# Query and value loads behind the block writes, a substitution begun in parts, and z in two pieces: a delta-rule layer with a maxout network on one core

## The chip, the core and the metric

The kernel runs on one core of a Trainium2 chip. Its time is the device time of one execution in microseconds (us); the number given for a kernel is the median of its runs. Profiles are taken by the hardware profiler on one execution. The engines are PE (TensorE; PEld is its weight load), DVE (VectorE), ACT (ScalarE), POOL (GpSimd) and SP (SyncE, which only issues DMAs). "L443" is line 443 of the kernel before. A change of 1% of the time (5 us) is about what a measurement of this kernel can tell from none.

## What is computed

Two layers one after the other. The first is a recurrence over 768 tokens for 4 batches x 8 heads, with a 48 x 48 state for each head (a delta rule); the second is a feed-forward network on its 3072 output rows of 384 numbers. In float32:

```python
k_n = k / (np.linalg.norm(k, axis=-1, keepdims=True) + 1e-06)
state = np.zeros((B, H, D, D), dtype=np.float32)
for t in range(S):
    kt, vt, bt = (k_n[:, :, t], v[:, :, t], beta[:, :, t, None])
    y[:, :, t] = np.einsum('bhd,bhde->bhe', q[:, :, t], state)
    v_old = np.einsum('bhde,bhd->bhe', state, kt)
    state = state + bt[:, :, :, None] * np.einsum('bhd,bhe->bhde', kt, vt - v_old)
...
x = y.transpose(0, 2, 1, 3).reshape(B * S, H * D)
h = np.maximum(np.maximum(x @ w1, x @ w2), x @ w3)     # 384 -> 768
return (h @ w_out).astype(np.float32)                  # 768 -> 384
```

## The kernel before, in words

**Chunks, units, groups.** The tokens are cut into 12 chunks of 64. A chunk has two units (one for each parity of the batch index; a unit holds 2 batches x 8 heads), so there are 24 units n = 0 to 23, and 6 groups m of two chunks each (512 tokens, four units). Inside a chunk the recurrence is solved in closed form: with the products of keys A = k k^T of a unit, a lower triangular system in blocks has to be inverted. Its 32 x 32 diagonal blocks are inverted by forward substitution on VectorE, for all blocks of a group at once, one block per partition; the rest is joined by small matmuls.

**Names of the steps.** For a unit n: `turn` (t, or T for queries alone) transposes keys and queries on TensorE (L366) and copies them out (L372); `gram` (g, or P for the products with queries alone) forms the products of keys and queries (L443); `to_dram` writes the key products to a scratch tensor at_d as eight block writes for two units (L473); `masked` (M) masks the query products (L427). For a group m: `blocks` gathers at_d with one block per partition (L544); `solve` runs the substitution; a run of it is advanced by hand, with one `yield` between its parts, as `some(solving, n)`, or S in the lists below. For a chunk c: `halves_z` and `halves_u` (e, f; only for the first two chunks, in 16 x 16 pieces), `turn_t1` (d, transposes on VectorE, L685 and L687), `join_z` (z, L768) and `join_u` (j, L781) complete the inverse `ut`; `old_k` (k, L798 and L810) and `old_q` (q, L798 and L818) apply the state; `new` (u, L826) forms the new values; `step` (s, L849 and L856) updates the state; `to_y` (y, L868 and L870) and `to_x` (x, L887) give the rows for the network. `scale` multiplies a chunk's values by the key norms (L324).

**The substitution** (L559 to 661). After the diagonal's inverse square root (L278 to L283) and the scaling by beta (L582), L599 scales the whole block matrix; the `yield` behind it ends the first part. Then come 31 steps j with two VectorE instructions each (L617 and L621), and one `yield` after each. For group 1 the result goes to the scratch tensor y_d (L641, two writes, one for each chunk) and is read back into `ut` in eight reads (L653, four for each chunk).

**Weights.** Each of 24 pieces is fetched as raw 64-bit words (`fetch`, L224, into five buffers), changed to float32 by three ScalarE instructions (L255 to L257, two sets of buffers), one on VectorE (L266) and one on POOL (L270, called by `join_last` or by the next piece).

**What sets the order.** Nothing is scheduled automatically: `tc.manual_schedule()` holds for the whole program, so each engine runs its instructions in the order in which the Python code makes them, and waits come from data and from buffers. The start-up (L1390 to L1472) handles group 0's keys and first chunk by hand. Then the network of group 0 is a generator, `ffn(0)`: each of its first 30 steps is one p_h, three accumulating products on 256 tokens (L1311, two passes each), followed by ScalarE (L1319, L1321) or VectorE (L1325); it has two buffers in PSUM. The body of the loop from L1558 runs after step i and hangs the other work there: the lists `FIRST` (chunk 1 and the solving of group 1), `EARLY_LINKS` (group 1), `SOLVED`, `FETCHED`, `CONVERTED` and `LESS`, in that order of calls. PSUM has three more buffers, `ps_two`, for all small products.

**The lines that the change touches.** `load_v(1)` stands at L1462 and is issued by POOL behind the weight fetch of L1461; `scale(1)` at L1562, in the body after step 0, with POOL; `load_q` for units 4 to 6 at L1564 to L1567, after steps 1 and 2, with SP. A q load writes one of three slots (`qpad[n % 3]`), so units 4, 5 and 6 go where units 1, 2 and 3 (the last in slot 0) were; their last readers are the transposes `turn(1..3, (1,))` of L1430 to L1435. `v_t` has three buffers.

Of the kernel before, what the change touches and what calls it, by code (L numbers as in the profile page):

```python
# [23 lines left out]
def kernel(  # L24
# [31 lines left out]
    nc = tc.nc  # L56
# [69 lines left out]
    def load(src, dst, n, queues):  # L126
        c, g = divmod(n, 2)
        for bb in range(2):
            queues[bb].dma_start(
                out=dst[rows(bb ^ g), :, 0:D],  # L130
                in_=src[2 * bb + g, :, c * C : (c + 1) * C, :].rearrange(
                    "h p d -> p h d"
                ),
            )
# [7 lines left out]
    def load_q(n, queues=one_queue):  # L142
        load(q, qpad[n % NQ], n, queues)

    def load_v(c, queue=nc.sync):
        vts[c] = work.tile([128, 2, H, D], FP32, name="v_t", bufs=3)
        for bb in range(2):
            queue.dma_start(  # L148
                out=vts[c][rows(bb)].rearrange("p g h d -> p (g h) d"),
                in_=v[2 * bb : 2 * bb + 2, :, c * C : (c + 1) * C, :].rearrange(  # L150
                    "b h p d -> p (b h) d"
                ),
            )
# [78 lines left out]
    def join_last():  # L232
        if waiting:
            joined(*waiting.pop())
# [88 lines left out]
    def scale(c, nrm):  # L323
        (nc.vector if c > 9 else nc.gpsimd).tensor_tensor(  # L324
            out=vts[c], in0=vts[c],
            in1=nrm[:, :, :, None].to_broadcast([128, 2, H, D]), op=ALU.mult,
        )
# [7 lines left out]
    nrm_0 = const.tile([128, 2, 2, H], FP32, name="nrm_0")  # L335
# [96 lines left out]
    def gram(n, parts=(0, 1), queues=one_queue, copy=nc.scalar.copy, later=False):  # L432
        kqt, g = kqts[n], n % 2
        p_g = ps_two("p_g")

        whole = len(parts) == 2 and not g
        for j in range(NP):
            for par in range(2):
                for bb in range(2):
                    kq = kqt[dims(par), j, bb ^ g]  # L440
                    for i in (0,) if whole else parts:
                        c0 = j * 128 + i * C
                        nc.tensor.matmul(  # L443
                            p_g[
                                rows(bb ^ (g * i)), par, c0 : c0 + C * (1 + whole)
                            ],
                            kq[:, 0],
                            kq if whole else kq[:, i],
                        )
        p_v = p_g.rearrange("p two (j i t) -> p two j i t", j=NP, i=2)  # L450
        if 1 in parts:
            pt = pts[n] = square("pt")
            if later:
                return lambda: copy(by_par(pt), p_v[:, :, :, 1])
            else:
                masked(pt, p_v[:, :, :, 1])
        if 0 not in parts:
            return
        at = ats[n] = square("at")
        copy(by_par(at), p_v[:, :, :, 0])  # L460
        if queues:
            to_dram(n, queues)
# [96 lines left out]
    def solve(m):  # L559
# [34 lines left out]
        else:  # L594
            size, xv, yv = BL, x[:, None], y[:, None]
            xb, by = x, bl[:, None, :].to_broadcast([128, BL, BL])
        if m == 2:
            yield
        nc.vector.tensor_tensor(out=xb, in0=xb, in1=by, op=ALU.mult)  # L599
        yield  # L600
        for j in range(size - 1):
# [5 lines left out]
            n = BL // size  # L607
# [86 lines left out]
    def halves_t(c, parts=(0, 1)):  # L694
        if c not in fine:
            fine[c] = [square("t") for g in range(2)]
        src = [ut[c % NU][:, g].rearrange("p h x -> p (h x)") for g in range(2)]
        dst = [t.rearrange("p h x -> p (h x)") for t in fine[c]]
        if 0 in parts:
            nc.vector.transpose(out=dst[0], in_=src[0])  # L700
        for bb in range(2) if 1 in parts else ():
            nc.vector.transpose(out=dst[1][rows(1 - bb)], in_=src[1][rows(bb)])
# [665 lines left out]
    def some(gen, n):  # L1368
        for _ in range(n):
            if next(gen, gen) is gen:  # L1370
                break
# [62 lines left out]
    some(conv, 1)  # L1434
    turn(3, (1,))  # L1435
    scores = [gram(n, (1,), None, later=True) for n in (2, 3)]
    some(solving, HB + 1)
    for copied in scores:
        copied()
# [15 lines left out]
    for n in range(2):  # L1455
# [3 lines left out]
    new(0)  # L1459
    some(conv, 1)  # L1460
    fetch(nc.gpsimd)  # L1461
    load_v(1, nc.gpsimd)  # L1462
    placed(1, 3)
    to_y(0)
    busy(2, ident)
    join_last()
    halves_t(1)
    solving = solve(1)
    some(solving, 1)
    to_x(0)  # L1470
# [27 lines left out]
    }  # L1498
    EARLY_LINKS = {
        9: "k0 q0", 10: "t0", 11: "t1", 12: "g0", 13: "t2", 14: "g1", 15: "t3",  # L1500
        16: "g2", 17: "g3", 20: "d0 d1 z0 z1", 22: "j0", 24: "j1 u0", 26: "s0",
        27: "y0", 28: "k1 q1", 29: "u1", 30: "s1 x0", 31: "y1",
    }


    FIRST = {
        0: "S1 S1", 1: "e1 s0 S1 S1 S1", 2: "f1 k1 M2 S1 S1",
        3: "z1 d1 S1 M3 S1 S1", 4: "j1 q1", 5: "u1 T4", 6: "y1 s1 T5", 7: "x1 T6",
        8: "T7", 14: "P4", 15: "P5", 23: "P6", 25: "P7", 30: "P9 P11",
    }  # L1510


# [26 lines left out]
    def queries(names):  # L1539
# [12 lines left out]
    FETCHED = {8: 1, 12: 1, 13: 1, 14: 1, 21: 2, 22: 1, 23: 1, 24: 1, 25: 1}  # L1552
    LESS = {3: 0, 6: 1, 9: 2, 18: 3, 21: 4, 25: 5}
    SOLVED = {
        **{i + 4: n for i, n in enumerate((3, 2, 2, 2, 3, 3, 3, 3, 2, 2))},
        27: 1, 28: 1, 29: 1, 30: 6, 31: 17, 32: 6, 33: 5,
    }
    for i, _ in enumerate(ffn(0)):  # L1558
        if i < 7:
            fetch(nc.sync if i else nc.gpsimd)  # L1560
        if i == 0:
            scale(1, nrm_0[:, 1])  # L1562
        if i == 1:
            load_q(4)  # L1564
            load_q(5)
        if i == 2:
            load_q(6)  # L1567
        if i < 6 or i == 16:
            join_last()
        for _ in range(FETCHED.get(i, 0)):  # L1570
            fetch(nc.gpsimd)
        queries(FIRST.get(i, ""))
        links(1, EARLY_LINKS.get(i, ""))
        if i == 26:
            solving = solve(2)
            some(solving, 1)
        if i in CONVERTED:
            some(conv, 1 + (i == 22))
        if i == 0:
            fetch(nc.gpsimd)  # L1580
        some(solving, SOLVED.get(i, 0))
        if i in (8, 13):
            prep_values(i // 4)
        if i in (4, 8):
            for n in range(2):
                load_k(8 + 2 * (i > 4) + n, (nc.gpsimd, nc.gpsimd))
        if i == 11:
            load_q(11, (nc.gpsimd, nc.gpsimd))
        if i in (3, 9, 10, 21):
            load_v((3, 9, 10, 21).index(i) + 2)  # L1590
        if i == 18:
            blocks(2)
        if i == 30:
            prep_values(4)
        if i in (29, 30, 31):
            load_blocks(i - 17, nc.sync)
        if i in LESS:
            less_first(LESS[i], nc.gpsimd if i < 10 else nc.vector)
        if i in (30, 31):
            turn_first((2 * i - 60, 2 * i - 59))  # L1600
        if i == 31:
            turn_first((4, 5))
            for t in range(KT):
                both_layers(t)
                if t == 0:
                    links(1, "x1")
# [55 lines left out]
```

## Time and profile before

| what | value |
|---|---|
| time, median of 3 runs | 500.26 us (500.18 to 503.68) |
| the profiled execution's own time | 500.94 us |
| its span, from first to last instruction | 499.2 us |
| mean granted clock of TensorE | 0.976 |
| busy, of the span | PE 96%, PEld 69%, DVE 70%, ACT 34%, POOL 40% |
| first p_h of the network (L1311) | 43.67 us |
| substitution of group 1, L599 to the last L621 | 46.14 to 86.50 us |
| its writes to y_d / first read of the read-back | 90.69 / 94.60 us |
| z of chunks 2 and 3 (L768) | 102.83 to 104.18 us |
| PE idle, 25 to 50 / 50 to 75 / 100 to 125 us | 5.06 / 4.37 / 1.17 us |
| PE idle, 125 to 495 us | none |

The profile gives for every instruction its start, duration and line, and for an engine's idle time what ended it ("<- DMA x": a transfer landed; "<- issue": nothing that the profile shows). Durations of PE are pipelined: a group's time is read from the start of one group to the start of the next. The share of the DMA engines is a mean over 16; it can pass 1 where packets overlap. The granted clock is 1.00 or 0.50 of full speed and changes at 5.16 us and from there on in steps of 3.41 us or a multiple of it: half from 29.05 to 42.70 and from 56.36 to 59.77 us.

### The profile page before, as it was taken

How to read it: one execution, taken by the hardware profiler on the slowest of the kernel's cores; microseconds unless marked ns; L12 is line 12 of the kernel's file. 1: busy time of each engine (PE TensorE's matmuls, PEld its weight loads, DVE VectorE, ACT ScalarE, POOL GpSimd, SP SyncE). 2: the span in 40 equal slices, each digit the busy share in tenths (PEclk: the TensorE clock that was granted, in tenths of full speed). 3: DMA queues.
4: the chain of work that ended last, by engine and by line, in shares of the span. 5: the costliest groups of instructions: out<-in, count | busy, mean ns of one | idle time of the engine just before them, and what ended most of it. 6: DMA issues, size and time to landing. Idle time of an engine off the chain costs nothing.

```text
span 499.2 us, 18774 instructions
## 1 busy us (share of the span) xinstructions
PE 479.1 (96%) x8100; PEld 343.1 (69%) x8100; DVE 350.6 (70%) x819; ACT 170.0 (34%) x329; POOL 199.4 (40%) x334
## 2 busy tenths in 40 slices
PE   7869799999999999999999999999999999999996
PEld 6658578887765556565554665555797456998896
DVE  5888879765588262799661999663999874468753
ACT  5676665986221133210135110234211032112310
POOL 7556683864770293882493790601000020000000
PEclk9767899999999999999999999999999999999999
DMA  8948969775350663546584554743224230330001
GB/s 110 166 100 221 201 178 131 195 182 131 83 144 6 137 133 84 138 117 151 119 156 99 127 135 114 152 78 89 67 49 92 53 85 12 87 84 16 1 16 47
DMA packets 109602, 53.51 MB, mean 107 GB/s; under 512 B 92752, under 2 KB 103344, under 8 KB 109520
## 3 DMA queue, kind: packets, MB, share of 16 engines
q1 hardware_dynamic: 97824, 31.62, 31.5%
q0 software_dynamic: 9280, 20.11, 16.1%
q8 instruction: 63, 1.03, 0.9%
q10 hardware_dynamic: 2416, 0.59, 0.7%
q14 instruction: 19, 0.16, 0.1%
HBM read 39.17 MB, written 13.11 MB: 105 GB/s over the span
## 4 chain that ended last, share of the span: by engine, by line
PE 91%; DVE 3%; issue 2%; ACT 2%; DMA 1%; SPq 0%; POOL 0%; DVEq 0%; ACTq 0%; POOLq 0%
PE p_h L1311 35%; PE p_o L1354 13%; PE p_o L1040 12%; PE p_c L1249 5%; PE p_g L443 4%; PE p_u L826 3%; PE p_y L868 3%; PE p_k L798 2%; PE p_m L960 2%; PE p_q L798 2%; PE p_s L849 2%; PE p_z L768 2%; PE p_j L781 2%; PE p_t L366 1%; PE p_e L1249 1%
## 5 line engine op out<-in xcount | busy, mean ns | idle before, releaser
L1311 PE MATMUL p_h<-xt,w_sb 128*128 128x512 f32 (+1 forms) x468 | 177.2, 523 | 0.3 <-ACT xt L894 0.3
L1311 PEld LDWEIGHTS p_h<-xt,w_sb 128*128 128x128 f32 x468 | 85.3, 191 | 62.7 <-issue 54.0
L1325 DVE TENSOR_TENSOR h<-h,p_h 128x512 f32<-128x512 f32 (+1 forms) x42 | 23.9, 569 | 44.3 <-PE p_h L1311 42.9
L621 DVE TENSOR_TENSOR y_bl<-y_bl,tmp 128x31 f32<-128x31 f32 (+20 forms) x139 | 48.7, 350 | 4.8
L617 DVE TENSOR_TENSOR tmp<-x_bl,y_bl 128x31 f32<-128x31 f32 (+20 forms) x139 | 48.9, 352 | 4.1
L1354 PE MATMUL p_o<-wo_sb,h 128*128 128x384 f32 x144 | 49.8, 491 | 0.0
L1321 ACT ACTIVATE h<-p_h 128x512 f32<-128x512 f32 (+1 forms) x30 | 16.6, 553 | 81.8 <-PE p_h L1311 75.8
L401 POOL DMA_DIRECT2D turned<-in_q_dram x72 | 39.3, 554 | 4.1 <-POOL turned L396 3.3
L1354 PEld LDWEIGHTS p_o<-wo_sb,h 128*128 128x128 f32 x144 | 26.7, 190 | 17.3
L443 PEld LDWEIGHTS p_g<-kqt 48*64 48x64 f32 x1184 | 23.5, 138 | 11.4 <-issue 6.9
L443 PE MATMUL p_g<-kqt 48*64 48x64 f32 (+1 forms) x1184 | 26.7, 238 | 2.8 <-ACT kqt L372 2.8
L270 POOL TENSOR_TENSOR w_sb<-mant,up 128x384 int32<-128x384 int32 x18 | 18.5, 1027 | 24.7 <-DVE mant L266 20.7
L653 POOL DMA_DIRECT2D ut<-y_d x4 | 2.6, 652 | 57.8 <-DMA y_d<-y_bl 57.8
L396 POOL MEMSET turned<- 128x96 f32 x18 | 3.3, 190 | 56.0 <-DVE kqt L417 56.0
L148 POOL DMA_DIRECT2D v_t<-in_v_dram x14 | 11.6, 832 | 34.5 <-PE p_u L826 34.5
L1360 ACT COPY o_sb<-p_o 128x384 f32<-128x384 f32 x12 | 5.7, 479 | 57.0 <-PE p_o L1354 51.6
L427 DVE TENSOR_TENSOR pt<-p_g,mask 128x512 f32<-128x512 f32 x20 | 13.6, 688 | 11.7 <-PE p_g L443 11.7
L1354 PE MATMUL p_o<-w_sb,xt 128*128 128x384 f32 x60 | 21.0, 486 | 0.0
L810 DVE TENSOR_TENSOR v_t<-v_t,p_k 128x768 f32<-128x768 f32 x11 | 10.5, 950 | 13.3 <-PE p_k L798 13.3
L460 ACT COPY at<-p_g 128x512 f32<-128x512 f32 x22 | 12.8, 585 | 19.6 <-DVE pt L427 17.2
L401 POOL DMA_DIRECT2D turned<-in_k_dram x32 | 17.5, 555 | 3.1 <-DMA v_t<-in_v_dram 1.7
L826 PEld LDWEIGHTS p_u<-v_t,ut 64*64 64x64 f32 x768 | 13.3, 142 | 6.7 <-issue 6.1
(254 smaller groups left out, 924.4 us busy)
## 6 DMA issues: line engine op xcount, KB each, us to landing
w_bits<-in_moe_w_dram SPq DMA_DIRECT2D x9, 384.0 KB, 5.2
w_bits<-in_moe_w_dram POOLq DMA_DIRECT2D x9, 384.0 KB, 5.9
turned<-in_q_dram POOLq DMA_DIRECT2D x72, 48.0 KB, 2.5
out_dram<-o_sb SPq DMA_DIRECT2D x34, 96.0 KB, 2.3
y_x<-y SPq DMA_DIRECT2D x30, 96.0 KB, 2.3
qall<-y_x SPq DMA_DIRECT2D x30, 96.0 KB, 2.8
v_t<-in_v_dram POOLq DMA_DIRECT2D x14, 192.0 KB, 5.2
at_d<-at SPq DMA_DIRECT2D x76, 32.0 KB, 2.9
```

The lines of the kernel that those rows point to most:

```text
L270: nc.gpsimd.tensor_tensor(out=dst.bitcast(I32), in0=mant_v.bitcast(I32), in1=up_v, op=ALU.add)
L401: (queue, nc.gpsimd)[i].dma_start(out=t[p0 : p0 + 32, bb, at : at + NP * 2 * D].rearrange("p (j x) -> p j x", j=NP), in_=(k, q)[i][2 * bb ...
L443: nc.tensor.matmul(p_g[rows(bb ^ (g * i)), par, c0 : c0 + C * (1 + whole)], kq[:, 0], kq if whole else kq[:, i],)
L617: nc.vector.tensor_tensor(out=t_v, in0=row.to_broadcast(t_v.shape), in1=column.to_broadcast(t_v.shape), op=ALU.mult,)
L621: nc.vector.tensor_tensor(out=rest, in0=rest, in1=t_v, op=ALU.subtract)
L798: nc.tensor.matmul(p_b[rows(bb), par, c0 : c0 + D], kqt[g][dims(par), j, bb ^ g, i], st[dims(par), bb ^ g, g, j],)
L826: nc.tensor.matmul(p_v[rows(bb ^ g), g, i], ut[c % NU][rows(bb), g, h], rhs[rows(bb), g, h],)
L1040: nc.tensor.matmul(to[:, g], a[j][:, 128 * g : 128 * (g + 1)], b[j], start=(start and g == of[0] and j == 0), stop=(stop and g == of[-1] a ...
L1249: nc.tensor.matmul(to, w[stays], moves, start=(n == 0), stop=(n == len(terms) - 1))
L1311: nc.tensor.matmul(p_h, w_sb[i][:, t, f * 128 : (f + 1) * 128], xt[:, t, lo : lo + w], start=(t == 0), stop=(t == KT - 1),)
L1325: nc.vector.tensor_tensor(out=h, in0=h, in1=p_h, op=ALU.max)
L1354: nc.tensor.matmul(p_o, stays, moves, start=(n == 0), stop=(n == len(terms) - 1))
```

## The change

Four things are moved; no instruction of arithmetic is added or taken away.

1. The values of chunk 1 (two DMAs) are asked for by SP instead of POOL, and much earlier in the program: in the start-up, behind the block writes of units 6 and 7. The queries of units 4, 5 and 6 (six DMAs) follow them on SP; they leave the bodies after steps 1 and 2.
2. `scale(1)` moves from the body after step 0 to the start-up, between a weight join and `halves_t(1)`; POOL now runs it ahead of the norm of group 1's substitution (L286 to L292).
3. The substitution of group 1 gets a second `yield` ahead of L599, so that its first part ends before the scaling. The lists call it otherwise: nothing after step 0, then three parts after each of steps 1, 2 and 3, four and three after steps 4 and 5 (before: two, three, two, three, three, two). From there on the same steps are done as before. On VectorE, L599 now stands behind the L1325 of step 1 and two L266; the step update L856 of chunk 0 directly behind L599 and ahead of the first step; three of the steps that stood ahead of L810 of chunk 1 stand behind it.
4. In `EARLY_LINKS`, z of chunk 2 follows step 19 and z of chunk 3 step 20, with a p_h between them (before, both followed step 20). j, u, s, y, k, q and u of chunk 3 then come one step earlier, x of chunk 2 goes ahead of the first p_o, and the two products P6 and P7 of `FIRST` come one step earlier.

```diff
@@ solve
-        if m == 2:
+        if m in (1, 2):
             yield
         nc.vector.tensor_tensor(out=xb, in0=xb, in1=by, op=ALU.mult)
         yield
@@ start-up
     scores = [gram(n, (1,), None, later=True) for n in (2, 3)]
+    load_v(1)
+    for n in (4, 5, 6):
+        load_q(n)
     some(solving, HB + 1)
...
     fetch(nc.gpsimd)
-    load_v(1, nc.gpsimd)
     placed(1, 3)
     to_y(0)
     busy(2, ident)
     join_last()
+    scale(1, nrm_0[:, 1])
     halves_t(1)
@@ lists
-        16: "g2", 17: "g3", 20: "d0 d1 z0 z1", 22: "j0", 24: "j1 u0", 26: "s0",
-        27: "y0", 28: "k1 q1", 29: "u1", 30: "s1 x0", 31: "y1",
+        16: "g2", 17: "g3", 19: "d0 z0", 20: "d1 z1", 21: "j0", 22: "j1", 23: "u0",
+        25: "s0", 26: "y0", 27: "k1 q1", 28: "u1", 29: "x0", 30: "s1", 31: "y1",
...
-        0: "S1 S1", 1: "e1 s0 S1 S1 S1", 2: "f1 k1 M2 S1 S1",
+        1: "e1 S1 s0 S1 S1", 2: "f1 k1 S1 S1 S1 M2",
         3: "z1 d1 S1 M3 S1 S1", 4: "j1 q1", 5: "u1 T4", 6: "y1 s1 T5", 7: "x1 T6",
-        8: "T7", 14: "P4", 15: "P5", 23: "P6", 25: "P7", 30: "P9 P11",
+        8: "T7", 14: "P4", 15: "P5", 22: "P6", 24: "P7", 30: "P9 P11",
...
-        **{i + 4: n for i, n in enumerate((3, 2, 2, 2, 3, 3, 3, 3, 2, 2))},
+        **{i + 4: n for i, n in enumerate((4, 3, 2, 2, 3, 3, 3, 3, 2, 2))},
@@ loop of ffn(0)
-        if i == 0:
-            scale(1, nrm_0[:, 1])
-        if i == 1:
-            load_q(4)
-            load_q(5)
-        if i == 2:
-            load_q(6)
```

## The prediction

> **What bounds the kernel now.** I read the page first, then TensorE's waits, then the timelines of TensorE and VectorE from 38 to 100 us, then tables of short windows. The page's first part, clock line and queue list:
>
> ```profile
> PE 479.1 (96%) x8100; PEld 343.1 (69%) x8100; DVE 350.6 (70%) x819; ACT 170.0 (34%) x329; POOL 199.4 (40%) x334
> PEclk9767899999999999999999999999999999999999
> q8 instruction: 63, 1.03, 0.9%
> ```
>
> PE is the bound: 479.1 of 499.2 us. The windows put its idle time before 137 us and after 495; from 125 to 400 us it is busy throughout. So only idle time or half clock before 137 us can be won. TensorE's waits, whole span (total, times, longest, in us):
>
> ```profile
> PE p_k L798 <- issue: 2.1, 1, 2.1
> PE p_u L826 <- issue: 1.2, 2, 1.0
> PE p_j L781 <- issue: 1.0, 1, 1.0
> PE p_y L868 <- issue: 0.8, 1, 0.8
> PE p_s L849 <- issue: 0.7, 2, 0.5
> ```
>
> "issue" means that nothing in the profile is waited for. The timeline of PE shows where (start, duration, then xcount, then idle before):
>
> ```profile
> 49.05 0.31 PE L849 MATMUL p_s<-u,kpad 64*64 64x48 f32 x2 [0.51 <-issue]
> 49.29 1.56 PE L1311 MATMUL p_h<-xt,w_sb 128*128 128x256 f32 x6
> 50.78 1.14 PE L751 MATMUL p_f<-z,t 64*64 64x32 f32 x64
> 51.73 1.01 PE L798 MATMUL p_k<-st,kqt 48*64 48x48 f32 x55
> 54.89 0.37 PE L798 MATMUL p_k<-st,kqt 48*64 48x48 f32 x9 [2.14 <-issue]
> ...
> 61.86 0.39 PE L781 MATMUL p_j<-z,t 32*32 32x32 f32 x23 [0.98 <-issue]
> ...
> 66.56 0.68 PE L826 MATMUL p_u<-v_t,ut 64*64 64x48 f32 x30 [1.04 <-issue]
> ```
>
> The stops cut groups at odd counts and come 2+6+64+55 = 127 matmuls apart (then 126, 127, and 127 again to a 0.21 us stop at 70.76). Queue q8 carries 1.03 MB in 63 packets: 16.4 KB each, for 16,200 loads and matmuls, or 257 instructions a packet. So these are stops for program code: one packet is used up before the next has come. Now the load (window, length, busy of PE, PEld, DVE, ACT, POOL, then clock, DMA share, GB/s):
>
> ```profile
> 33.00:34.00 1.00, 0.21 (x5) 0.09 (x2) 0.67 (x3) 0.90 (x5) 1.00 (x2) 0.50 0.00 0
> 37.00:38.00 1.00, 0.82 (x32) 0.85 (x35) 0.89 (x2) 0.46 (x2) 1.00 (x2) 0.50 0.60 197
> 53.00:54.00 1.00, 0.00 (x0) 0.00 (x0) 1.00 (x1) 0.99 (x4) 0.90 (x1) 1.00 1.04 263
> 57.00:58.00 1.00, 1.00 (x66) 0.94 (x65) 0.90 (x4) 0.37 (x1) 0.00 (x0) 0.50 1.08 295
> ```
>
> The long stop lies in saturated DMA, the DMA engines are empty at 33, and after the stop the clock is halved from 56.36 to 59.77 us. VectorE's timeline shows the second chain, which holds the second substitution (L617, L621):
>
> ```profile
> 52.76 1.37 DVE L266 TENSOR_SCALAR mant<-mant 128x384 uint32<-128x384 uint32 x1
> 55.30 0.95 DVE L810 TENSOR_TENSOR v_t<-v_t,p_k 128x768 f32<-128x768 f32 x1 [1.17 <-PE p_k L798]
> 70.27 0.95 DVE L870 TENSOR_TENSOR y<-qs,p_y 128x768 f32<-128x768 f32 x1 [1.97 <-PE p_y L868]
> 71.63 0.95 DVE L856 TENSOR_TENSOR st<-st,p_s 128x768 f32<-128x768 f32 x1 [0.41 <-PE p_s L849]
> ```
>
> From 46 to 87 us it has almost no other idle time, so PE can only run ahead of it by a little.
>
> **The early loads.** Eight DMAs move: v of chunk 1 (2 x 192 KB, POOL, 42.26 to 43.93) and q of units 4 to 6 (6 x 96 KB, SP, 45.75 to 52.02) go behind SP's last block write, which issues until 30.73. The same forms issue in about 0.65 us each, so they issue from 30.75 to 36 us. Their buffers are free by then: the last reader of the three q slots, the transposes of unit 3, is done by 24.2 us. The first k loads, with the same 192 B runs, moved 160 to 200 GB/s, so 960 KB takes 5 to 6 us and ends near 37.5 us. Nothing queues behind them on SP until the weight fetch at 45.1. The gather of the next blocks (POOL, 36.04, landed 3.6 us later) shares up to 1.5 us with their tail. ScalarE uses it at 40.49 and then has 1.07 us idle before L894, so I take 0 for it (39.66 + 1.5 is 0.7 us past 40.49, inside that idle time; bounds 0 and 0.7).
>
> POOL loses 1.67 us of issuing, and scale(1) (L324, 1.64 us, until now at 49.52 after a 0.96 us wait for v) goes ahead of the norm (L286). It would run at about 43.3 to 44.8; the norm needs VectorE's L283 (45.70), so it keeps its place. The weight join at 51.13 comes about 2.6 us earlier, and with it ScalarE's L255, which waited 3.9 us for it. On PE's path: 0, since p_h at 55.26 had its weights from 52.13.
>
> **TensorE, ledger of 44 to 71 us.** Removable: stops 0.51 + 2.14 + 0.98 + 1.04 + 0.21 = 4.88; half clock, p_z 0.17 + p_h 2.38 instead of 1.49 + 0.2 = 1.3. Together 6.2 us. What comes late next:
> - The j1 matmuls need the transposes d1 of VectorE. VectorE afterwards: L586 ends 46.1, L266, L1325, L266 to 47.2, L599 (1.22) to 48.4, then L856 must wait for p_s (48.9 to 49.4), so it ends at about 50.1; two steps and the four L318 (1.75), L1325 and L266 (0.65) to 52.5; L810 waits for p_k, at 52.4 without a stop, 53.1 with 0.7 us left of it; the three postponed steps 1.75, L427 and L266 1.0, d1 1.37: 57.2 to 57.9. PE would be there at 56.3. About 1.2 us is given back.
> - VectorE gains by the end of the substitution: 1.17 + 1.0 (L266 at 1.37 against 0.35, beside POOL's join) + 1.97 + 0.41 = 4.55, less the new wait for p_s (0.5 to 1.0) and what is left of that for p_k and the join (0 to 1.9): 1.7 to 4.0, and I take 2.75.
> - PE ahead of that: p_h at 91.22 needs a buffer that ScalarE's L1321 frees at 90.46, in a queue behind VectorE's L427; slack 0.76. So PE stands 2.75 + 0.76 = 3.5 us earlier there (2.5 to 4.8).
>
> **Substitution in parts.** An extra yield and other counts put L599 behind L1325 and two L266, and three steps behind L810; by step 5 of the loop the counts agree again. The work is the same, 0 us beyond the waits above.
>
> **z in two pieces, and its followers one step earlier.** z0 goes before the p_h of step 20, where it would have stood at 101.5 in today's time, z1 at 103.5. The DMA view gives the read-back of the first chunk landed by 99.5, of the second by 101.9 (issue at 99.35 plus 2.5). These follow VectorE, so they move 2.75 earlier; slack 2.0 and 1.6 is more than 0.76, hence no wait. The weights of steps 18 to 20 (joins until 98.4) had 3.1 us and move with VectorE too. The count of matmuls is unchanged: 0 us. The two code stops at 120.58 and 124.59 (0.85 + 0.32) lie in the same dense y, k, q groups; I take 0, with bounds -1.2 (both gone) and +1.0 (one more like that at 66.56).
>
> **The price at the new place.** The packet used from 37.8 us (127 matmuls before 46.15: 24 matmuls into the first p_u) is fetched at about 35.1, in empty DMA engines:
>
> ```profile
> q8 instruction: 1, 0.02, 6.3%
> ```
>
> (window 34.9 to 36.0). Data end to use is 1.6 us there, and 1.3 to 1.6 us at the stops, so this packet has no reserve. It now meets the q loads. From the last crossing to the packet's start took 0.7 us there, 1.0 to 1.5 us beside 192 B loads alone (9.76, 79.7 us), up to 5.6 us beside mixed loads (19.56). I take 0.4 us of stop, with bounds 0 and 5.2.
>
> **Sum.** -3.5 + 0.4 = -3.1 us. The profiled execution took 500.94 us (499.2 span and 1.74 around it): 497.84 by its own time. It stood 0.68 above the median of 500.26, so the median after is 497.2.
>
> **Rules weighed.** The Trainium skill, "Runtime: NRT & Kernel Launch", section "Instruction fetch mechanics", says that code comes in 16 KiB blocks of 256 instructions through a queue of the sequencer, and that crossing a block is mostly hidden; the block agrees with the trace (16.4 KB, 257), the hiding does not (2.14 us at 54.89). By that rule the stops are something else and stay, so the sum would be 0 (rival 3 below gives it from rows).
> The windows from 35.87 to 39.29 us show PE 92% busy, yet the clock stays at 0.50 until 42.70; the next window, 100% busy and with 128x128 matmuls of L1385 in it, releases it. The Trainium skill, "TensorE: Matmul & The Clock Gate", section "What's actually happening", has one busy window of about 3.4 us release the clock; by it 92% would have done, and the 1.2 us of rival 2 would be 0. The trace disagrees, so I keep the 1.2.
>
> **Rivals.**
> 1. All stops go, also those at 119 to 125, and VectorE is never blocked: 4.55 + 0.76 + 1.17 = 6.5 at most, about 5.6 after the wait for p_s (0.5 to 1.0): 494.7 us. For it: the load at 44 to 54 loses 960 KB of 2.15 MB. Against it: dense groups eat a packet in 3.4 us even without load, and the stop at 124.59 came with little load.
> 2. Slower: the stop moves to p_u at 37.8. Every us of it is paid, for p_u, p_y, L872, p_x and p_h follow each other to 43.67. A stop past 39.29 (over 1.5 us) also takes the fully busy window away, and p_h runs at half clock until 46.11: 2.44/2 = 1.2 us more. It decides from a stop of about 2.3 us. With 5.2 + 1.2 and no gain 506.7; with gain 503.2; middle 503.
> 3. It doesn't do what it says: the weight fetches fill the freed DMA time (five buffers, all asked for as they come free), or the stops come from something other than DMA load; they stay: 500.0 us.
>
> **Numbers.** Forecast 0.48, own range 495.0 to 498.6 (2.5 less 0.8 of stop, to 4.8 and a part of the 1.2), with 0.07 below 495.3; rival 1 0.23; rival 2 0.15, half of it past 505.3; rival 3 0.14. 1% is 5.0 us, about what a measurement of this kernel can tell from no change. Faster by over 1%: 0.23 + 0.07 = 0.30; slower: 0.08; within: 0.62. 494.2 to 501.0 leaves out half of rival 1 and most of rival 2.
>
> **What would show it.** Right: "issue" before p_k under 0.8 us, no half clock after 56 us, DMA busy from 32 to 37, d1 the last releaser of p_j, L870 without its 1.97 us. Wrong: "issue" before p_u near 38 us over 1.5 us, the clock released at 46 instead of 42.7, or a wait of p_z for the read-back.

## The result, and the profile after

| | before | after |
|---|---|---|
| median, runs of the first comparison | 500.42 us (22 runs) | 503.06 us (22 runs) |
| ratio, 95% interval | | 1.0054 [1.0031, 1.0077] |
| profiled execution: own time / span | 500.94 / 499.2 us | 505.39 / 503.6 us |
| mean granted clock | 0.976 | 0.974 |

The changed kernel is slower, by about half a per cent (2.6 us), where 3.1 us less had been forecast; 503.06 also lies outside the range. Two later comparisons of the same kernel gave 1.0040 [1.0012, 1.0067] and 1.0029 [0.9995, 1.0064]. Executions over 1.5% longer than a kernel's fastest are left out of the ratios; the profiled ones of runs 12 and 17 below are of that kind.

Part of the profiled difference arises ahead of the first instruction that was moved (the loads of the values, at 31.54 us in after). The group p_e starts at 26.98 us in the profile of before and at 29.82 in that of after, and in 20 profiles of all kernels of this study it starts either at 26.9 to 27.6 us (14 of them) or at 29.6 to 29.9 (6, of six kernels). One kernel does both: the changed one started p_e at 29.82, 27.49 and 27.07 in its three profiles. All six late ones are among the 12 profiles of kernels that have both the early loads and the second `yield`, none among the other eight; whether the change makes the late start more frequent is not shown. In any case absolute times of the two traces must not be subtracted. Below, stretches are measured from an event inside the trace: from VectorE's L280 (the last step of the norm but one) or from the first p_h.

The page of after: busy time of PE, its clock in 40 slices, and the queue of program code.

```profile
PE 483.7 (96%) x8100; PEld 346.9 (69%) x8100; DVE 349.8 (69%) x819; ACT 170.2 (34%) x329; POOL 196.8 (39%) x332
PEclk9956899999999999999999999999999999999999
q8 instruction: 64, 1.05, 0.9%
```

PE's waits in after (total us, times, longest). The first is new, the other three answer to those of p_k, p_u and p_y before:

```profile
PE p_t L366 <- DVE y L870: 2.5, 1, 2.5
...
PE p_k L798 <- issue: 1.3, 1, 1.3
...
PE p_u L826 <- issue: 0.6, 2, 0.4
...
PE p_y L868 <- issue: 0.5, 1, 0.5
```

The stops for code are smaller: p_k 1.3 instead of 2.1, p_u 0.6 instead of 1.2, p_y 0.5 instead of 0.8, and those in p_j and p_s are gone. At the top stands a wait that before did not have: the query transposes T5 (L366) wait 2.5 us for VectorE's L870. PE's timeline (start, duration, count, idle before):

```profile
40.02 0.88 PE L826 MATMUL p_u<-v_t,ut 64*64 64x48 f32 x23 [0.18 <-issue]
41.35 1.32 PE L826 MATMUL p_u<-v_t,ut 64*64 64x48 f32 x41 [0.44 <-issue]
...
47.45 3.01 PE L1311 MATMUL p_h<-xt,w_sb 128*128 128x256 f32 x12
...
54.85 1.01 PE L798 MATMUL p_k<-st,kqt 48*64 48x48 f32 x55
57.18 0.37 PE L798 MATMUL p_k<-st,kqt 48*64 48x48 f32 x9 [1.32 <-issue]
57.48 2.41 PE L1311 MATMUL p_h<-xt,w_sb 128*128 128x256 f32 x6
...
68.83 1.15 PE L868 MATMUL p_y<-u,pt 64*64 64x48 f32 x64
69.80 1.11 PE L849 MATMUL p_s<-u,kpad 64*64 64x48 f32 x64
73.38 0.66 PE L366 MATMUL p_t<-ident,qall 128*128 128x128 f32 x4 [2.47 <-DVE y L870]
```

The same p_y before:

```profile
69.06 1.15 PE L868 MATMUL p_y<-u,pt 64*64 64x48 f32 x64
```

From the first p_h to p_y (y1) PE takes 68.83 - 47.45 = 21.4 us; before it took 69.06 - 43.67 = 25.4. So PE did come 4.0 us ahead here; the ledger of the prediction had 6.2 less 1.2, so 5.0 (0.2 of it behind p_y). Then it stops for 2.5 us. T5 starts 0.05 us after L870's end (72.39 + 0.94 = 73.33): the small products take turns in three PSUM buffers, and the one that T5 gets is freed by L870, which reads p_y. VectorE's timeline says why L870 is late:

```profile
48.39 0.19 DVE L280 SCALAR_TENSOR_TENSOR nt_bl<-root_bl,nt_bl 128x32 f32<-128x32 f32 x1
...
50.57 0.42 DVE L1325 TENSOR_TENSOR h<-h,p_h 128x256 f32<-128x256 f32 x1 [0.82 <-PE p_h L1311]
50.91 1.32 DVE L266 TENSOR_SCALAR mant<-mant 128x384 uint32<-128x384 uint32 x1
52.15 1.21 DVE L599 TENSOR_TENSOR wo_sb<-wo_sb,inv_bl 128x1024 f32<-128x1024 f32 x1
53.28 0.94 DVE L856 TENSOR_TENSOR st<-st,p_s 128x768 f32<-128x768 f32 x1
...
57.58 0.95 DVE L810 TENSOR_TENSOR v_t<-v_t,p_k 128x768 f32<-128x768 f32 x1 [1.17 <-PE p_k L798]
58.46 0.24 DVE L617 TENSOR_TENSOR tmp<-wo_sb,y_p 128x87 f32<-128x87 f32 x1
...
72.39 0.94 DVE L870 TENSOR_TENSOR y<-qs,p_y 128x768 f32<-128x768 f32 x1
```

The first two of these before:

```profile
45.12 0.19 DVE L280 SCALAR_TENSOR_TENSOR nt_bl<-root_bl,nt_bl 128x32 f32<-128x32 f32 x1
46.14 1.22 DVE L599 TENSOR_TENSOR wo_sb<-wo_sb,inv_bl 128x1024 f32<-128x1024 f32 x1
```

L599 starts 52.15 - 48.39 = 3.76 us behind L280; before it was 46.14 - 45.12 = 1.02. It starts 2.7 us later. Of these, 0.9 are the L1325 and the two L266 that now stand ahead of it, work that is only done earlier. The other 1.8 are lost: VectorE stands idle for 0.82 us in front of L1325, which waits for the first p_h, and behind that L266 takes 1.32 us instead of 0.35, beside POOL's join:

```profile
50.99 1.01 POOL L270 TENSOR_TENSOR w_sb<-mant,up 128x384 int32<-128x384 int32 x1
```

L266 ends 0.23 us after this join does. Further on, L810 waits 1.17 us for p_k, and the three steps that could have filled that wait (L617 at 58.46 is the first) stand behind it. L870 has no wait of its own any more. The forecast had counted on that (1.97 us gone), but here it went because VectorE itself is late.

### The profile page after: what moved, and what is told of

It is laid out like the page before. It is cut to its first block, busy times and chain, and to the rows that moved or that the text cites. A ratio compares the mean times of both kernels' runs of the same rounds, so it can differ in the third digit from the quotient of the medians.

```text
span 503.6 us, 18776 instructions
## 1 busy us (share of the span) xinstructions
PE 483.7 (96%) x8100; PEld 346.9 (69%) x8100; DVE 349.8 (69%) x819; ACT 170.2 (34%) x329; POOL 196.8 (39%) x332
## 4 chain that ended last, share of the span: by engine, by line
PE 87%; DVE 6%; DMA 2%; SPq 2%; issue 1%; ACT 1%; POOL 0%; ACTq 0%; POOLq 0%
PE p_h L1311 33%; PE p_o L1354 13%; PE p_o L1040 12%; PE p_c L1249 5%; PE p_g L443 4%; PE p_u L826 3%; PE p_y L868 2%; PE p_k L798 2%; PE p_m L960 2%; PE p_q L798 2%; PE p_s L849 2%; DVE tmp L617 2%; SPq L129 2%; PE p_j L781 1%; PE p_z L768 1%
## 5 line engine op out<-in xcount | busy, mean ns | idle before, releaser
L1325 DVE TENSOR_TENSOR h<-h,p_h 128x512 f32<-128x512 f32 (+1 forms) x42 | 23.9, 569 | 46.0 <-PE p_h L1311 45.2
L617 DVE TENSOR_TENSOR tmp<-x_bl,y_bl 128x31 f32<-128x31 f32 (+20 forms) x139 | 49.0, 353 | 4.1
L443 PEld LDWEIGHTS p_g<-kqt 48*64 48x64 f32 x1184 | 25.0, 147 | 11.6 <-issue 7.7
L443 PE MATMUL p_g<-kqt 48*64 48x64 f32 (+1 forms) x1184 | 28.6, 248 | 2.2 <-ACT kqt L372 1.9
L270 POOL TENSOR_TENSOR w_sb<-mant,up 128x384 int32<-128x384 int32 x18 | 18.9, 1049 | 28.4 <-DVE mant L266 22.7
L148 POOL DMA_DIRECT2D v_t<-in_v_dram x12 | 9.9, 830 | 34.4 <-PE p_u L826 34.4
L427 DVE TENSOR_TENSOR pt<-p_g,mask 128x512 f32<-128x512 f32 x20 | 13.6, 688 | 10.8 <-PE p_g L443 10.6
L810 DVE TENSOR_TENSOR v_t<-v_t,p_k 128x768 f32<-128x768 f32 x11 | 10.5, 950 | 13.4 <-PE p_k L798 13.4
L856 DVE TENSOR_TENSOR st<-st,p_s 48x768 f32<-48x768 f32 (+1 forms) x18 | 17.1, 949 | 1.1 <-PE p_s L849 0.7
```

What stands on the lines that cost most here:

```text
L270: nc.gpsimd.tensor_tensor(out=dst.bitcast(I32), in0=mant_v.bitcast(I32), in1=up_v, op=ALU.add)
L443: nc.tensor.matmul(p_g[rows(bb ^ (g * i)), par, c0 : c0 + C * (1 + whole)], kq[:, 0], kq if whole else kq[:, i],)
L617: nc.vector.tensor_tensor(out=t_v, in0=row.to_broadcast(t_v.shape), in1=column.to_broadcast(t_v.shape), op=ALU.mult,)
L856: nc.vector.tensor_tensor(out=s_v[r], in0=s_v[r], in1=p_s[r, :, 0 : H * D], op=ALU.add)
L1325: nc.vector.tensor_tensor(out=h, in0=h, in1=p_h, op=ALU.max)
```

## The experiments

Three theories. **S**: the new order of the substitution on VectorE costs it (L599 behind L1325, three steps behind L810, so L870 and the substitution's end are late). **L**: the early loads meet TensorE's code fetch ahead of the first p_h. **Z**: z in two pieces costs it. Later two more were needed: **C**, a code packet among the last writes, and the stop at T5 with the clock behind it.

| run | kernel | median | before | ratio [95%] |
|---|---|---|---|---|
| 1 | early loads only | 498.42 | 499.63 | 0.9985 [0.9960, 1.0010] |
| 2 | substitution's order only | 501.53 | 499.63 | 1.0025 [0.9999, 1.0051] |
| 3 | z in two pieces only | 501.14 | 499.63 | 1.0026 [0.9990, 1.0062] |
| 4 | early loads and z | 499.75 | 499.63 | 0.9973 [0.9941, 1.0004] |
| 5 | changed kernel again | 503.03 | 501.21 | 1.0040 [1.0012, 1.0067] |
| 6 | changed kernel, z as before | 501.81 | 501.21 | 1.0012 [0.9981, 1.0043] |
| 7 | changed kernel, three steps ahead of L810 | 501.42 | 501.21 | 1.0016 [0.9985, 1.0046] |
| 8 | as 7, and L599 ahead of L1325 | 500.01 | 501.21 | 0.9984 [0.9960, 1.0008] |
| 9 | changed kernel, T5 one step later | 501.91 | 501.44 | 1.0023 [0.9997, 1.0049] |
| 10 | as 8, z as before | 501.03 | 501.44 | 0.9997 [0.9967, 1.0026] |
| 11 | early queries only | 499.97 | 501.44 | 0.9975 [0.9946, 1.0003] |
| 12 | early values and scaling only | 501.45 | 501.44 | 0.9977 [0.9943, 1.0012] |
| 13 | changed kernel, third time | 503.63 | 501.95 | 1.0029 [0.9995, 1.0064] |
| 14 | changed kernel, 8 code words more | 504.31 | 501.95 | 1.0034 [1.0002, 1.0067] |
| 15 | changed kernel, 64 code words more | 509.64 | 501.95 | 1.0148 [1.0099, 1.0197] |
| 16 | as 8, 8 code words more | 500.18 | 501.95 | 0.9976 [0.9945, 1.0007] |
| 17 | as 8, T5 one step later | 499.88 | 500.55 | 0.9995 [0.9968, 1.0021] |
| 18 | early loads, T5 one step later | 498.63 | 500.55 | 0.9970 [0.9941, 1.0000] |

The interval of one comparison is 0.23 to 0.5% to each side, as wide as most single effects; what is read below are differences between kernels that were measured side by side (1 to 4, 5 to 8, 9 to 12, 13 to 16, 17 and 18), and what several comparisons agree on. The ratio is not the quotient of the two medians: for run 4 the medians give 1.0002 and for run 12 1.0000, where the ratios are 0.9973 and 0.9977; for the others the two are within 0.0014. Runs 12 and 17 are read by their times alone.

### 1 to 4: the parts one by one

Run 1 is the kernel before with parts 1 and 2 of the change:

```diff
     scores = [gram(n, (1,), None, later=True) for n in (2, 3)]
+    load_v(1)
+    for n in (4, 5, 6):
+        load_q(n)
...
-    load_v(1, nc.gpsimd)
...
     join_last()
+    scale(1, nrm_0[:, 1])
...
```

> The kernel before with the early loads alone (v of chunk 1 and q of units 4 to 6 on SP behind the block writes, scale(1) ahead of the norm); substitution and z as before. Theory L (the loads meet the code fetch for p_u near 38 us, and the clock comes back later): 2 to 3 us slower than before, a stop of 0.4 us or more inside the first p_u. Theory S (the loss is the substitution's: L599 behind L1325, VectorE late at L870): the loads alone win 1 to 3 us, 497.5 to 499.5, with the stop before p_k at 1.3 us or less. Theory Z (z earlier costs): as S.

Run 2 is the kernel before with part 3:

```diff
-        if m == 2:
+        if m in (1, 2):
...
-        0: "S1 S1", 1: "e1 s0 S1 S1 S1", 2: "f1 k1 M2 S1 S1",
+        1: "e1 S1 s0 S1 S1", 2: "f1 k1 S1 S1 S1 M2",
...
```

> The kernel before with the substitution in parts alone (second yield, the lists of steps 0 to 5). Theory S: 2 to 3 us slower, L870 of chunk 1 more than 1 us later against L280 than before, and the transposes of unit 5 wait for it. Theories L and Z: within 0.5 us of before.

Run 3 is the kernel before with part 4 (the new `EARLY_LINKS`, P6 and P7 a step earlier), run 4 all of the change but part 3.

> The kernel before with z in two pieces and its followers one step earlier alone. Theory Z (z of chunk 2 or its followers wait for the read-back or for VectorE, or the code stops at 111 to 126 us grow): 0.5 to 2.5 us slower. Theories L and S: within 0.5 us of before; z at 101.5 has 2.0 us of slack to the read-back.

> All of the change but the substitution in parts. Theory S: faster than before by 1 to 3 us, and by 3.5 to 5.5 than the changed kernel. Theory L: 2 to 3 us slower than before, as the changed kernel. Theory Z: 0.5 to 2.5 us slower than the early loads alone.

Measured: by their ratios only the kernels with early loads and the old order lie below 1 (runs 1 and 4); the order alone, and z alone, lie above it. All four intervals hold 1. The order's cost is seen best where p_k stops longest. VectorE's row of run 2:

```profile
56.38 0.95 DVE L810 TENSOR_TENSOR v_t<-v_t,p_k 128x768 f32<-128x768 f32 x1 [3.71 <-PE p_k L798]
```

Before, the same wait was 1.17 us: p_k's own stop was 3.24 us here instead of 2.14, and the three steps that had stood in front of L810 no longer use the time. It follows that theory L alone is out: it asked for 2 to 3 us of loss from the early loads, and neither run with them shows any. How S and Z share the loss was open.

### 5 to 8: undoing the order in the changed kernel

Run 5 is the changed kernel again, run 6 without part 4. Runs 7 and 8 change the lists of the changed kernel, 7 the entry of step 2 alone, 8 all of it:

```diff
     solving = solve(1)
-    some(solving, 1)
+    some(solving, 2)
...
-        1: "e1 S1 s0 S1 S1", 2: "f1 k1 S1 S1 S1 M2",
+        1: "e1 s0 S1 S1", 2: "f1 S1 S1 S1 k1 M2",
```

> The changed kernel once more, beside the next three on one chip, as their mark: 2 to 3.5 us slower than before. Theory S (VectorE waits at L810 and L1325 with steps of the substitution behind it): L280 to L870 of chunk 1 lasts about 24 us, of which 2 us or more is idle. Theory L expects the loss ahead of the first p_h.

> The change without z in two pieces (early loads and substitution in parts). If the parts of the change simply add up (loads -1.2, parts +1.3 to 1.9, z +1.3 to 1.5 in the medians so far): 0 to +0.7 us against before, 499.6 to 500.4. If the parts cost more beside the early loads (theory S with PE ahead of VectorE): +1.5 to +3 us, with the transposes of unit 5 waiting 1.5 to 2.5 us for L870.

> The changed kernel, but the three steps after step 2 of the loop stand ahead of k1 again, so VectorE has them to do while it waits for p_k at L810. Theory S: L810's idle time falls from 1.2 to 3 us to under 0.6, L870 1 to 2 us earlier, 1 to 2.5 us faster than the changed kernel. Theory L or Z: no change against it.

> As the one before, and L599 stands again at the end of the first part, ahead of L1325: the substitution has its old order on VectorE up to the norm's transposes, with early loads and z in two pieces. Theory S: 2 to 4 us faster than the changed kernel, as the loads with z in two pieces (499.8 median, 1.3 us faster than before by the ratio). Theory L or Z: no change against the changed kernel.

Measured side by side on one chip: 503.03 for the changed kernel, 501.42 with the three steps put back, 500.01 with L599 put back too. So undoing the order in these two places alone gives 3.0 us, with all loads and z as changed. That is theory S. It is not the old order in full: L856 of chunk 0 still stands ahead of the first step, and no step stands ahead of the first L1325. Run 6, without z in pieces, took 501.81, 1.2 us less than run 5, while T5 waited 2.65 us in it; so z could be a part of the loss as well.

### 9 to 12: the stop at T5, z, and which load it is

Run 9 moves T5 in the changed kernel; runs 10 to 12 are as in the table.

```diff
-        3: "z1 d1 S1 M3 S1 S1", 4: "j1 q1", 5: "u1 T4", 6: "y1 s1 T5", 7: "x1 T6",
+        3: "z1 d1 S1 M3 S1 S1", 4: "j1 q1", 5: "u1 T4", 6: "y1 s1", 7: "x1 T5 T6",
```

> The changed kernel, but the query transposes T5 (L366) follow step 7 of the network instead of step 6; nothing on VectorE's list changes place. Ratio of the changed kernel to the one before, so far: 1.0040 and 1.0054. Theory S1 (what TensorE loses is mainly the stop of T5 for the row result L870, 2.5 us, with the half clock that follows it): the stop goes, ratio 1.000 or less (2 us or more won). Theory S2 (the late substitution is what TensorE pays; T5 is only where it shows first): TensorE goes on to the p_h behind it and stops one product later for a buffer that a late VectorE frees, so under 1 us is won: 1.003 to 1.005.

> The change without z in two pieces (old list of links), with the scaling L599 ahead of L1325 and the three steps ahead of L810 again, as in the run before that undid both (ratio 0.9984 with z in two pieces). If z in two pieces costs the 0.26 to 0.28% that two comparisons gave, 0.9956 (2.2 us faster than before); if it costs nothing, 0.998 to 0.999, and then no version here beats the kernel before by more than 0.3%.

> Kernel before with only the six query loads on SP behind the block writes; values and their scaling as before. With both loads moved the ratio was 0.9985. If the queries are what empties the DMA engines between 44 and 54 us: stop ahead of p_k under 1.3 us (before 2.14), 0.998. If the values and the earlier scaling (which takes 1.6 us of POOL from beside VectorE's L266) win it: 1.000, stop of p_k as before.

> Kernel before with only the values of chunk 1 on SP and their scaling ahead of the norm; query loads as before. If the values and the scaling win: 0.9985, VectorE's L280 to L870 about 2 us shorter, stop of p_k about as before. If the queries do: 1.000. In both cases the stop in the first p_u near 38 to 41 us is under 0.5 us, since only 384 KB are early (theory L: the code packet meets the query loads).

Measured: run 9 fell between the two theories (1.0023, 0.0017 below run 5, which was measured apart from it, and inside the intervals). In its profile p_x waits 0.98 us for L870 and T5 0.32 us for ScalarE, so half of the stop comes back at once. Run 10 speaks against Z where the order is undone: without z in pieces the version of run 8 is no better (0.9997 against 0.9984). Runs 11 and 12 gave the same, so neither load is singled out.

### 13 to 16: is it the tail?

By now the profiles had shown something else: in two profiles of the changed kernel the span ended 5.8 and 5.6 us after the last matmul, in all others 3.75 to 4.0. The transfers after the last matmul, first of after, with the median time from issue to landing in the last column:

```profile
q8 instruction: 1, 0.02, 1.6%
...
out_dram<-o_sb SPq DMA_DIRECT2D x2, 48.0 KB, 2.9
out_dram<-o_sb ACTq DMA_DIRECT2D x2, 48.0 KB, 4.1
```

and of run 13, the same program:

```profile
out_dram<-o_sb ACTq DMA_DIRECT2D x2, 48.0 KB, 2.0
out_dram<-o_sb SPq DMA_DIRECT2D x2, 48.0 KB, 2.0
```

In after a packet of TensorE's code (q8) is moved among the last output writes, and 15 packets of these land 0.8 to 1.7 us behind all others of their queue. Runs 14 to 16 shift TensorE's code late in the program by products that nobody reads:

```diff
         for i, _ in enumerate(ffn(m)):
+            if i == 0 and m == GROUPS - 2:
+                busy(2, ident[:, 0:2])      # run 15: busy(16, ...)
```

> The changed kernel once more, as the measure of the next three. If the code packet among the last writes belongs to this program: from the last matmul to the end of the span 5.6 to 5.8 us as in its two other profiles (all other kernels 3.75 to 4.0), ratio 1.004 to 1.005. If it was chance: 4.0 us.

> The changed kernel with two products of two columns more on TensorE ahead of the second-last part of the network (they go to a buffer that nobody reads): its code from there on is shifted by 8 instructions. Theory C (the packet among the last writes costs 1.8 us): if the packet moves out of the tail, end of the span 4.0 us after the last matmul and ratio 1.000 to 1.001; if it stays, as the changed kernel. Theory S (the substitution's order costs all of it): ratio 1.004 to 1.005 in both cases.

> As the run before, with sixteen products of two columns: the code is shifted by 64 instructions, some 5 us ahead of the end at the rate of the last products; the products cost up to 0.8 us. Theory C: the packet lies ahead of the last writes, 4.0 us from the last matmul to the end, ratio 1.001 to 1.002 with that cost. Theory S: 1.005 to 1.006.

> The version with the substitution's order undone (L599 ahead of L1325 and three steps ahead of L810; 0.9984) with the same two products more. Theory C: if the packet comes among the last writes here, 5.6 us from the last matmul to the end and ratio 1.002; if not, 4.0 us and 0.998 to 0.999. Theory S: 0.998 to 0.999 in both cases.

Measured: the changed kernel's third profile ended 3.99 us after the last matmul, and run 14 too, yet their ratios stayed at 1.0029 and 1.0034. Run 18 had the packet in its tail (5.7 us) with a ratio of 0.9970. So theory C does not account for the order's price: the packet costs 1.6 to 1.8 us where it comes, but it came in three of 20 profiles, of two kernels, one of them below 1. It is not out as a small part of the loss: the profiled execution of run 13, without it, was the fastest of that run's 12 (499.40, median 503.63), and one profile does not tell how often the packet comes. Run 16 repeats run 8: 0.9976, so the order undone gives 0.0055 of the ratio (2.8 us) against runs 13 and 14 beside it. Its VectorE rows, to be held against those of after:

```profile
48.34 0.19 DVE L280 SCALAR_TENSOR_TENSOR nt_bl<-root_bl,nt_bl 128x32 f32<-128x32 f32 x1
...
49.35 1.22 DVE L599 TENSOR_TENSOR wo_sb<-wo_sb,inv_bl 128x1024 f32<-128x1024 f32 x1
...
50.78 0.40 DVE L1325 TENSOR_TENSOR h<-h,p_h 128x256 f32<-128x256 f32 x1
51.10 1.94 DVE L266 TENSOR_SCALAR mant<-mant 128x384 uint32<-128x384 uint32 x1
...
57.75 0.94 DVE L810 TENSOR_TENSOR v_t<-v_t,p_k 128x768 f32<-128x768 f32 x1
```

L599 runs while p_h is still being made, L1325 has no wait, and L810 none. In PE's rows T5 follows with a stop of 0.14 us, too short for the view to show; in run 8, with the same order, it stops for 2.0:

```profile
72.88 0.66 PE L366 MATMUL p_t<-ident,qall 128*128 128x128 f32 x4
```

```profile
71.70 0.66 PE L366 MATMUL p_t<-ident,qall 128*128 128x128 f32 x4 [2.01 <-DVE y L870]
```

Yet L870 starts 22.5 us behind L280 in run 8 and 23.5 in run 16. PE is what differs: in run 16 the clock is at half from 62.07 to 68.90 us, ahead of T5, and PE comes to it later. So the stop at T5 tells how far PE is ahead of VectorE, not only how late L870 is.

Run 15 missed every forecast (1.0148); what it showed stands in the last section.

### 17 and 18: T5 once more

> The version with the substitution's order undone, with the query transposes T5 one step later as well. If the stop at T5 and the half clock behind it are what a late L870 costs, they cannot occur: no half clock between 60 and 100 us, L870 to the last step of the substitution 15.6 us (17.25 where the clock was halved), ratio 0.995 to 0.997. If not: 0.998, as without it.

> Kernel before with the early loads alone (0.9985) and T5 one step later. Its stop at T5 was 0.6 us in the one profile, too short for a half clock: 0.997 to 0.999, little or no change from the early loads alone.

Measured: with the order undone, T5's place makes no difference that these runs can tell (0.9995 against 0.9984 and 0.9976), nor with the loads alone (0.9970 against 0.9985). The stop at T5 is a symptom, and moving it is no cure. No version beats the kernel before by a difference clear of its interval; the nine with early loads (or a part of them) and the order old or undone (runs 1, 4, 8, 10, 11, 12, 16, 17 and 18) lie 0.03 to 0.30% below it by their ratios.

## Why the prediction was wrong

**The step that failed** is "Substitution in parts", with its "The work is the same, 0 us beyond the waits above". The profiles of all kernels with early queries, in us, mean and range; both stretches go from start to start:

| | order old (runs 1, 4, 11, 18) or undone (8, 10, 16) | new order: after, runs 5, 6, 9, 13, 14, 15 |
|---|---|---|
| L280 to L870 of chunk 1 | 22.8 (22.3 to 23.8) | 24.0 (23.7 to 24.4) |
| L280 to the last step of the substitution | 38.8 (37.9 to 39.7) | 40.6 (39.5 to 41.7) |
| stop of PE at T5 | 0.1 to 0.6; 2.0 in run 8 | 1.7 to 2.65; 0.3 in run 9, with T5 moved |
| half clock right after it | run 8 | runs 5, 6, 14, 15 |

Before, the second stretch took 41.18 us, and in run 3, which is the same kernel up to there, 40.25. So with the order of the first column the early loads win 1.5 to 2.4 us of VectorE's chain, where 2.75 was forecast; with the new one at most 0.6 is left. The order takes 1.8 us by the profiles (1.15 if the new one is held against runs 8, 10 and 16 alone, which average 39.4) and 2.8 to 3.0 by the times (runs 8 and 16). So 1 us or more of it has no place in the rows, and stays open.

What the step had overlooked, point by point:
- It put L599 behind L1325 at the times of before, where the first p_h is ready for it. With the loads, p_h comes later, and L1325 with L599 behind it waits 0.6 to 0.8 us (after, runs 5 and 15; 0.1 to 0.9 in the seven profiles). An instruction that needs nothing new was queued behind one that does.
- "1.0 (L266 at 1.37 against 0.35, beside POOL's join)" was booked as won. The join comes earlier, but so does VectorE to it: L266 still takes 1.32 in after (1.48 in run 5), and in runs 7 and 14 it is L599 itself that lies there and takes 3.07 us instead of 1.21. In the old order that time fell behind L599 (run 16).
- PE's stop before p_k was to shrink to 0.7 us or less; it was 1.32, and VectorE's wait for p_k is 1.17 again (1.61 in run 5), with three steps of 1.75 us together behind it.
- L870 was not followed to TensorE. The j1 wait for d1 was priced, the buffer of p_y for T5 was not. A stop of PE at T5 was in no rival.

**The half clock behind it.** In four of the seven profiles with the new order (and in runs 7 and 8) the clock is halved right after T5. Windows of run 5 (length, busy of PE, PEld, DVE, ACT, POOL, then granted clock, DMA share, GB/s):

```profile
69.00:72.40 3.40, 0.83 (x25) 0.71 (x18) 3.26 (x7) 0.00 (x0) 3.38 (x5) 1.00 0.85 173
72.40:75.80 3.40, 3.40 (x12) 2.76 (x12) 2.51 (x7) 0.58 (x1) 3.40 (x5) 0.50 0.72 183
75.80:79.20 3.40, 3.40 (x22) 3.09 (x21) 2.59 (x8) 1.88 (x3) 2.52 (x3) 1.00 0.83 154
```

and of after, whose clock steps fall otherwise:

```profile
68.27:71.68 3.41, 2.64 (x131) 2.16 (x130) 3.24 (x9) 1.85 (x5) 3.07 (x5) 1.00 1.00 171
71.68:75.09 3.41, 1.71 (x10) 1.58 (x11) 3.31 (x7) 0.59 (x1) 3.39 (x5) 1.00 0.81 165
```

The same stop of 2.5 us lies within one step of the clock in run 5 (PE busy 0.83 of 3.40) and is cut in two in after (2.64 and 1.71 of 3.41); only the first halves the clock. The window with the stop held 0.76 to 1.41 us of busy PE in the six profiles that were halved, and 1.71 in after and 1.72 in run 13, which were not. VectorE then waits for the halved p_h: from L870 to the end of the substitution it takes 17.25 us in run 5 and 15.58 in after, 1.7 us more. The Trainium skill, "TensorE: Matmul & The Clock Gate", section "What's actually happening", has free-running windows of 3413 ns and the throttled state after one idle window; the trace agrees with both, and shows that a window that counts as idle need not be empty.

**The early loads** did part of what was said: u1 and y1 come without stops, and the DMA engines are at work from 34 us on. But "issue" before p_k, forecast under 0.8 us, was 1.32 in after, 0.64 in run 16 and about 1.7 in runs 1, 5, 13 and 15. Their price ahead of the first p_h was put at 0.4 us; from the first p_u to the first p_h the 15 profiles with early queries that are read here take 7.31 us on average (6.8 to 7.8), and before and runs 2 and 3 take 6.5, 6.5 and 6.0, so it is 0.95 by the means. The stop in p_u is 0.1 to 1.2 us (0.35 to 0.8 in 12 of them), well under the 2.3 of the second rival. In six of the 15 (after, runs 1, 4, 5, 9 and 15) the clock was released 17.2 to 18.0 us behind p_e's start, in the other nine 15.2 to 16.4, and in before 15.7. That rival had the place right and the size wrong. **"No half clock after 56 us"** failed in after too (58.04 to 61.45).

**z in two pieces** was put at 0. By the ratios it showed +0.26% alone (run 3) and +0.28% in the changed kernel (run 5 against 6), but -0.12% with the loads (4 against 1) and -0.13% with the order undone (8 against 10). By the medians of the same pairs three of these are a loss, of 1.5, 1.2 and 1.3 us (4 against 1 too), and the last is a gain of 1.0. They do not agree, so a price of about 1 us is neither shown nor out; the read-back held z up in one of the profiles read here, by 0.33 us (run 9).

**The sum.** Forecast -3.5 + 0.4. Measured in the profiles: VectorE's gain 0.6 instead of 2.75, with the slack of 0.76 at most 1.4, and the price 0.95: from -0.4 to +0.3. The times say +1.5 to +2.7. With the order undone and the rest as changed (runs 8 and 16) they say -0.8 to -1.2, so the sign turns on the failed step; of its size, 1 us or more stays unexplained. TensorE's rows do not show it: from p_e's start to the last matmul the changed kernel took 468.0, 469.6 and 466.6 us (after, runs 5 and 13), runs 8, 10 and 16 took 467.1, 468.6 and 467.8, and before and run 3 468.5 and 466.0. The profiles of one kernel differ by as much as what is sought. Left as rivals are z, and a late start-up or a late last write that comes oftener in one kernel than in another; one profile of a kernel cannot tell that.

**The range** failed because its slow side held one mechanism only, the code packet. A reordering priced at 0 had no bounds at all.

## What to carry to other kernels

An edit that "only reorders" an in-order engine has a price: for each instruction that moves, ask what now stands in front of it, when that becomes ready in the new timeline (not the old one), and which work no longer fills which wait. Then follow the late result to whoever waits for its buffer. A wait that vanishes may only say that the waiter has become late; and with an interval of 0.25% for a comparison, pairs run side by side and stretches measured from an event inside the trace tell more than spans.

## What the runs showed of the hardware

- **A busy PE on the page is not always a busy PE to the clock.** In after, the window ahead of the half clock at 58.04 us has more busy time than the one at 71.68 shown above (1.71), which left the clock alone:

```profile
54.63:58.04 3.41, 2.09 (x95) 1.86 (x88) 2.14 (x9) 2.88 (x7) 1.00 (x1) 1.00 1.05 284
```

  Its products are those of p_f and p_k mostly (64x32 and 48x48), the other's are 128x128 weights with 128 and 256 columns. Run 15 is the extreme: 32 passes with 128x128 weights and two columns take 3.63 us (0.11 us each, from 384.26 to 387.89 us), 48x48 products follow them, PE counts as busy throughout the first of these windows, and still the next is at half:

```profile
386.00:389.40 3.40, 3.40 (x125) 3.38 (x127) 0.64 (x2) 0.00 (x0) 0.00 (x0) 1.00 0.51 97
389.40:392.80 3.40, 3.40 (x39) 1.79 (x32) 2.17 (x5) 0.80 (x1) 0.00 (x0) 0.51 0.77 139
```

  The 14 products that run 15 has more than run 14 cost 3.1 us and the half clock 1.7, together 4.8 of the 5.7 us (0.0114) between the two.
- **VectorE beside POOL's join.** L266 takes 0.29 to 0.61 us in the 382 cases that overlap no join (POOL's L270); of the 98 in the 20 profiles that overlap one none ends before it, and 78 end 0.2 us after it (52.23 against 52.00 in after). Those near 50 us that start ahead of the join took 1.25 to 1.95 us. L599 took 3.07 instead of 1.21 there, in runs 7 and 14. The other way round, POOL's L289 takes 1.24 us beside L599 (before) and 0.37 in after. The Trainium skill, "SBUF — State Buffer", section "SBUF: two separate sides", says that some of VectorE's operations and GpSimd's share a pair of ports under an exclusive lock, so that the loser blocks; these rows agree, though they do not tell who took the lock first (L266 starts 0.08 us ahead of the join in after).
- **A code packet among the last writes** delayed the end by 1.6 to 1.8 us in three of 20 profiles, in one execution of a program and not in the next.
- **Start-up comes in two lengths** 2 to 3 us apart, in the same program. The eight profiled executions with the late start-up or with the packet in the tail took 1.1 to 5.3 us more than their kernel's median, the other twelve from 4.2 less to 1.9 more. That is a part of why single executions of one kernel differ by up to 10.6 us (before, beside runs 1 to 4).
